# Attention and two MoE layers on one core: reciprocals a head later, transfers and opening in another order, the cosine's integer from ScalarE in the first block

## The chip, the cores and the metric

One core of a Trainium2 chip runs the whole program. The metric is the time of one execution in microseconds (us) on the device; lower is better. The kernel before takes 2205.02 us (median of three runs, 2204.62 to 2205.92).

## The reference

Three layers in a row, all in float32. Attention has 4 batches of 8 heads, 576 tokens of 64 numbers each, with a mask by blocks of 64. Its output, 2304 tokens of 512 numbers, goes through a layer with a cosine (512 to 2048 and back), and that through eight experts with a gate.

```python
scores = 0.125 * np.matmul(q, k.transpose(0, 1, 3, 2))
scores = np.where(mask, scores, -1e9)
attn = np.exp(scores - scores.max(-1, keepdims=True))
attn = attn / (attn.sum(-1, keepdims=True) + 1e-09)
x = np.matmul(attn, v)          # -> 2304 x 512
h = x @ w_in                    # first MoE
x = (h * np.cos(h)) @ w_out
...
for e in range(8):              # second MoE, P from a normalised gate
    out += P[:, e:e + 1] * (np.maximum(x @ w1[e], 0) @ w2[e])
```

## The kernel before

The whole program is written in a fixed order: each engine executes its instructions in the order in which the Python code records them, and waits on semaphores for the others. All transfers of the attention are issued by SyncE (SP in the profile), one after the other; an issue that has to wait holds up all behind it, and each waits until the eighth transfer ahead of it has landed.

**Attention** goes head by head (line 408, 32 heads). Precision is bought by splitting each float32 number into a high part and a low part. For head i the loop does, in this order: it evacuates the output of head i-1 from PSUM (`evac`, ScalarE) and sends its row of sums to DRAM (`sums`); it sends the high part of the next head's q to its place (`move_q_hi`, `qb<-qa`); TensorE makes the first half of the next head's peaks (`peak(i+1, 0)`, tile `px`) and VectorE finds their maxima (`find`, tile `nm`); TensorE makes the scores of head i (`weights`, tiles `sp`, `sq`, `sr`, `sc`), ScalarE their exponentials; then the second half of the peaks and its `find`. The two halves share one `px` in PSUM, so the second half waits for the first `find`. For head i+2, `high_parts` and `low_parts` split q and k, and `move_k_hi`, `move_k_lo` (`kb<-hi`, `kb<-qb`) send parts of k to other partitions. `move_q_hi` of a head overwrites what `move_k_lo` of it reads, so it waits for that transfer to land. Then come the products with v (`pv`, tile `o`), and between them the maxima of head i+1 are transposed (`turn`, tile `pt`) and written into `qa` (`maxima`, line 286); the scores of head i+1 wait for that.

Two heads make one pair, an even head and an odd one. The sums of a pair are fetched from DRAM in another layout (`fetch`, `sc<-sums`), inverted (`invert`, line 358, on VectorE), sent back (`give`), spread over the partitions (`spread`, `tt<-inv`), and the outputs are scaled by them (`scale`, one head each, line 375); `x_hi` on ScalarE and `x_lo` on GpSimd (POOL) split the result into `xh` and `xl`. `fetch`, `invert` stand in the even head, `give` and `spread` in the next odd one.

Beside this runs the conversion of the first MoE's weights from float64 to float32 (`Conv`, tiles `cw`, `tla`, `raw`): 32 halves, each in four steps, of which `some(n)` lets n run. Half of them run in the attention, one in each pair of heads, the rest in the first block of the first MoE.

**The first MoE** takes 3 blocks of 16 units. A unit makes two tiles of h (24 matmuls, `h<-xh,jh`), takes their cosine, and the unit after it multiplies the result by the second weights (`o_part`, `acc`). The cosine is ScalarE's Sin of h minus whole turns: `reduce_h` gets the integer `ki` and the rest `r` on VectorE, `sine` runs on ScalarE, `times` and `g_lo` on VectorE. Two tiles of h fit in PSUM, so a third waits for `times` of the first. The last pairs of the attention are finished in the first units (`leftover`). **The second MoE** follows from some 680 us to the end and is not touched.

## Time and profile before

| | |
|---|---|
| median of three runs | 2205.02 us |
| profiled execution, its own time | 2205.72 us |
| span of its trace, first to last instruction | 2203.9 us |
| TensorE, VectorE, ScalarE, GpSimd busy | 98%, 68%, 43%, 39% of the span |
| TensorE busy in the first two slices of 55 us | 7 and 8 tenths, then 8, 8, 8, 9 and 9 to the end |
| mean granted TensorE clock | 0.993 of full speed |

The profile's page has the busy shares of each engine, the span in 40 slices, the chain of work that ended last, and the costliest groups of instructions. Behind it stand views of the trace: windows of time with the busy time of each engine, the waits by engine and releaser, and the instructions in order of time.

### The profile page before, as it was taken

Reading aid. Unit: us, or ns where it says so; the run is one execution under the profiler, and the core shown is the slowest. Engines: PE = TensorE matmul, PEld = TensorE weight load, DVE = VectorE, ACT = ScalarE, POOL = GpSimd, SP = SyncE. Lnnn points to the kernel's source line nnn. Section 1 sums busy time; section 2 is a strip of 40 time slices with the busy share of each in tenths; the row PEclk is TensorE's granted clock in tenths of the full one; section 3 lists DMA queues with packets and bytes.
Section 4 is the critical chain, followed back from the end, with each engine's and each line's share of the span. In section 5 each row is a group of like instructions: output and inputs, shape, how many; then the busy total and the mean of one; then the engine's idle time right before and its main releaser. Section 6 shows DMA issues by size and latency. Waiting matters only on the chain.

```text
span 2203.9 us, 29623 instructions
## 1 busy us (share of the span) xinstructions
PE 2150.4 (98%) x10869; PEld 1889.4 (86%) x10869; DVE 1497.8 (68%) x2464; ACT 957.5 (43%) x1792; POOL 867.5 (39%) x766
## 2 busy tenths in 40 slices
PE   7888899999999999999999999999999999999999
PEld 5666689999898888888888888888888888888887
DVE  6777688666566876666767666666777666666665
ACT  5666555434444343433434434343434343433342
POOL 1222355333332343434563434343554343434341
PEclk9999999999999999999999999999999999999999
DMA  5676421000001121212122212121212221212120
GB/s 144 173 181 175 112 73 58 1 1 10 29 20 39 58 77 58 77 58 77 58 77 87 77 58 77 58 77 58 77 58 88 76 77 58 77 58 77 58 77 29
DMA packets 76641, 157.42 MB, mean 71 GB/s; under 512 B 33392, under 2 KB 33392, under 8 KB 76496
## 3 DMA queue, kind: packets, MB, share of 16 engines
q1 hardware_dynamic: 76496, 155.52, 23.1%
q8 instruction: 86, 1.41, 0.3%
q14 instruction: 59, 0.48, 0.1%
HBM read 136.91 MB, written 4.87 MB: 64 GB/s over the span
## 4 chain that ended last, share of the span: by engine, by line
PE 77%; DVE 7%; issue 7%; DMA 3%; ACT 3%; POOL 3%; SPq 1%; ACTq 0%; POOLq 0%; DVEq 0%
PE acc L470 12%; PE acc L472 12%; PE acc L471 12%; PE hx L472 6%; PE hx L470 6%; PE hx L471 6%; PE hy L472 3%; PE hy L470 3%; PE hy L471 3%; PE acc L701 3%; POOL jl L66 3%; DMA kb<-qb 1%; PE hz L470 1%; PE hz L472 1%; PE hz L471 1%
## 5 line engine op out<-in xcount | busy, mean ns | idle before, releaser
L580 POOL TENSOR_TENSOR wv<-stg,wv 128x512 fp32r<-128x512 f32 x190 | 333.7, 1778 | 858.5 <-ACT wv L579 858.5
L470 PE MATMUL acc<-wv,hh 128*128 128x512 f32 x1152 | 456.5, 396 | 0.0
L472 PE MATMUL acc<-wv,hl 128*128 128x512 f32 x1152 | 455.5, 395 | 0.0
L471 PE MATMUL acc<-wv,hh 128*128 128x512 f32 x1152 | 454.5, 395 | 0.0
L874 DVE SCALAR_TENSOR_TENSOR oa<-acc,P,oa 128x512 f32<-128x512 f32 x540 | 379.0, 740 | 4.9 <-PE acc L472 4.3
L845 ACT ACTIVATE hh<-c 128x384 fp32r<-128x384 f32 x288 | 151.4, 526 | 408.7 <-DVE c L930 167.8
L846 DVE SCALAR_TENSOR_TENSOR hl<-c,hh 128x384 fp32r<-128x384 f32 x288 | 164.0, 570 | 176.5 <-ACT hh L845 176.5
L472 PEld LDWEIGHTS acc<-wv,hl 128*128 128x128 f32 x1152 | 216.0, 187 | 53.7
L471 PEld LDWEIGHTS acc<-wv,hh 128*128 128x128 f32 x1152 | 215.9, 187 | 43.8
L470 PEld LDWEIGHTS acc<-wv,hh 128*128 128x128 f32 x1152 | 216.1, 188 | 43.0
L66 POOL TENSOR_TENSOR jl<-raw,jh 128x512 fp32r<-128x512 f32 x95 | 135.4, 1443 | 240.5 <-ACT jh L63 225.9
L923 DVE TENSOR_TENSOR c<-hz,c 128x384 f32<-128x384 f32 x96 | 53.5, 557 | 193.2 <-PE hz L472 193.2
L571 DVE TENSOR_TENSOR wal<-s,wah 128x1024 fp32r<-128x1024 f32 x96 | 171.4, 1785 | 0.0
L913 ACT ACTIVATE c<-hx 128x384 f32<-128x384 f32 x95 | 46.9, 493 | 275.5 <-PE hx L472 275.5
L470 PE MATMUL h<-xh,jh 128*128 128x384 f32 x384 | 130.5, 340 | 5.7 <-ACT jh L63 3.0
L472 PE MATMUL h<-xh,jl 128*128 128x384 f32 x384 | 129.9, 338 | 1.9 <-POOL jl L66 1.9
L673 ACT ACTIVATE r<-r,half_pi 128x384 f32<-128x384 f32 x96 | 59.2, 617 | 165.5 <-DVE r L668 164.7
L472 PE MATMUL hy<-xh,wal 128*128 128x384 f32 x384 | 128.8, 335 | 0.9 <-DVE wal L571 0.9
L471 PE MATMUL h<-xl,jh 128*128 128x384 f32 x384 | 129.2, 337 | 0.0
L470 PE MATMUL hx<-th,wah 128*128 128x384 f32 x384 | 128.6, 335 | 0.5 <-ACT c L913 0.5
L470 PE MATMUL hy<-xh,wah 128*128 128x384 f32 x384 | 128.7, 335 | 0.4 <-DVE c L930 0.2
L472 PE MATMUL hx<-th,wal 128*128 128x384 f32 x384 | 128.5, 335 | 0.0
(213 smaller groups left out, 4822.1 us busy)
## 6 DMA issues: line engine op xcount, KB each, us to landing
stg<-in_w_b_dram SPq DMA_DIRECT2D x192, 512.0 KB
cw<-in_w_a_dram SPq DMA_DIRECT2D x32, 512.0 KB
st<-in_qk_dram SPq DMA_DIRECT2D x64, 144.0 KB
v<-in_v_dram SPq DMA_DIRECT2D x31, 160.0 KB
tt<-inv SPq DMA_DIRECT2D x32, 144.0 KB
out_dram<-oa SPq DMA_DIRECT2D x18, 256.0 KB
kb<-hi SPq DMA_DIRECT2D x31, 144.0 KB
kb<-qb SPq DMA_DIRECT2D x31, 144.0 KB
```

The source lines that it names most:

```text
L66: eng_lo.tensor_tensor(out=lo, in0=src, in1=hi.bitcast(F32), op=ALU.subtract)
L470: nc.tensor.matmul(ps, lh, rh, start=first, stop=False, skip_group_check=go_on)
L471: nc.tensor.matmul(ps, lh, rl, start=False, stop=False, skip_group_check=go_on)
L472: nc.tensor.matmul(ps, ll, rh, start=False, stop=last, skip_group_check=go_on)
L571: eng.tensor_tensor(out=self.al, in0=self.s, in1=self.ah.bitcast(F32), op=ALU.subtract)
L580: eng.tensor_tensor(out=t[:, DM:2 * DM], in0=src, in1=t[:, 0:DM].bitcast(F32), op=ALU.subtract)
L673: nc.scalar.activation(r, r, AF.Sin, bias=half_pi)
L701: nc.tensor.matmul(acc[half, b][:, at:at + w_], w[:, s], h[:, t0:t0 + w_], start=f == 0 and i == 0 and at == 0, stop=f == F1 - 1 and i == ...
L845: nc.scalar.activation(hh, src, AF.Relu)
L846: nc.vector.scalar_tensor_tensor(out=hl, in0=src, scalar=0.0, in1=hh.bitcast(F32), op0=ALU.max, op1=ALU.subtract)
L874: nc.vector.scalar_tensor_tensor(out=o, in0=acc, scalar=p, in1=o, op0=ALU.mult, op1=ALU.add)
L923: nc.vector.tensor_tensor(out=c[0], in0=z, in1=c[0], op=ALU.add)
```

## The change

In the attention, `invert` and `give` move from the even head to the next odd head, behind the first `find`; `scale` of an even head moves to the end of the even head, `x_hi` and `x_lo` follow one head later, and a third buffer of outputs holds the pair that long. On SyncE's queue the loads of v, q and k come first in a head, then `sums` and `move_q_hi`; `fetch` and `spread` change places around `move_k_hi` and `move_k_lo`. The four steps of a conversion are cut differently. In the opening, GpSimd writes the constants of the second slot and the ones beside v, and VectorE makes `maxima(0)` ahead of `low_parts(1)`. The first weights of the first MoE are split during the last head, into a corner of `xh` and `xl` that is not yet written, and those of unit 1 ahead of unit 0. The left-over pairs are spread over units 1 to 9 instead of 0 to 5. In the 16 units of the first block, ScalarE makes the integer `ki`.

```diff
...
-            def constants(slots):
...
+            def constants(j, eng):
+                eng.tensor_copy(out=QA[j][:, 0:64], in_=diag[:, 0:64])
+                eng.tensor_copy(out=QA[j][64:96, 64:640], in_=diag[64:96, 64:640])
+                eng.tensor_scalar(out=KA[j][64:128, :], in0=diag[64:128, 0:S], scalar1=0.0, scalar2=None,
+                                  op0=ALU.mult)
...
+            def ones_of_v():
+                nc.gpsimd.memset(V[0][:, :, D:D + 1], 1.0)
+                nc.gpsimd.memset(V[1][:, :, 0:D], 0.0)
...
...
                 self.magnitude(k)
-                self.rounding(k)
                 if 0 < k < NHALF - 1:
                     self.load(k + 1)
                 yield
+                self.rounding(k)
                 self.clamp(k)
                 yield
                 self.shift(k)
+                self.bits(k)
                 yield
-                self.bits(k)
                 self.add(k)
                 yield
...
-            constants([0])
+            selectors()
+            constants(0, nc.vector)
+            constants(1, nc.gpsimd)
             first_head()
-            find(*peak(0, 0))
+            px = peak(0, 0)
+            tiles()
+            find(*px)
             find(*peak(0, 1))
-            constants([1])
             high_parts(1)
-            low_parts(1)
-            more_constants()
...
+            ones_of_v()
             turn(0)
             maxima(0)
+            low_parts(1)
...
                 if i:
                     evac(i - 1)
-                if odd and i >= 3:
-                    give(i - 3)
+                    if nxt:
+                        load_v(i + 1)
+                if i + 3 < NH:
+                    load(i + 3)
                 if i:
                     sums(i - 1)
+                if even and i:
+                    some(1)
                 if nxt:
                     move_q_hi(i + 1)
-                if i and nxt:
-                    load_v(i + 1)
-                if nxt:
                     find(*peak(i + 1, 0))
                 for part in range(4):
                     weights(i, part)
-                if i >= 4:
-                    scale(i - 4 - i % 2, i % 2)
+                if odd and i >= 3:
+                    invert(i - 3)
+                    give(i - 3)
+                if odd and i >= 5:
+                    scale(i - 5, 1)
                 if nxt:
                     find(*peak(i + 1, 1))
+                if nxt2:
+                    high_parts(i + 2)
+                    move_k_hi(i + 2)
+                if even and i >= 2:
+                    fetch(i - 2)
+                if nxt2:
+                    low_parts(i + 2)
+                    move_k_lo(i + 2)
                 if odd and i >= 3:
                     spread(i - 3)
-                if i + 3 < NH:
-                    load(i + 3)
-                if even and i >= 2:
-                    fetch(i - 2)
-                if i + 2 < NH:
-                    high_parts(i + 2)
-                    move_k_hi(i + 2)
-                    low_parts(i + 2)
-                    move_k_lo(i + 2)
-                if even:
-                    some(1)
-                elif i >= 5:
-                    x_hi(i - 5)
-                    x_lo(i - 5)
-                if even and i >= 2:
-                    invert(i - 2)
-                if odd:
-                    some(1)
+                if even and i >= 6:
+                    x_hi(i - 6)
+                    x_lo(i - 6)
+                if i == NH - 1:
+                    split(*spare, raw[0][:, 0:DM], nc.scalar, nc.gpsimd)
+                some(1)
                 pv(i, 0)
                 pv(i, 1)
...
                 for c in range(2, 5):
                     pv(i, c)
-                some(1)
+                if even and i >= 4:
+                    scale(i - 4, 0)
+                if odd:
+                    some(1)
...
-                    nc.vector.tensor_scalar(out=ki, in0=ps, scalar1=float(1 / TWO_PI), scalar2=0.25,
-                                            op0=ALU.mult, op1=ALU.add)
+                    if n < F1:
+                        nc.scalar.activation(ki, ps, AF.Identity, bias=quarter, scale=float(1 / TWO_PI))
+                    else:
+                        nc.vector.tensor_scalar(out=ki, in0=ps, scalar1=float(1 / TWO_PI), scalar2=0.25,
+                                                op0=ALU.mult, op1=ALU.add)
...
-                wsplit(0, 0, nc.vector)
+                wj[0, 0] = spare
...
+                        if n == 0:
+                            wsplit(1, 0)
```

What a pair of heads is on VectorE. First before: the end of an even head, from the step of the conversion that `bits` is, with the numbers of the tiles (`nm_106`, `qa_97` and so on are the two slots that even and odd heads use).

```order
L119 SCALAR_TENSOR_TENSOR raw<-cw,tla 128x512
L277 TENSOR_REDUCE nm_106<-px 128x1 x2
L375 TENSOR_TENSOR tt<-tla,tt 64x576
L277 TENSOR_REDUCE nm_106<-px 128x1 x3
L233 TENSOR_TENSOR qb_100<-st,hi 128x576
L358 RECIPROCAL sc_116<-sc_116 72x16
L286 TENSOR_TENSOR qa_97<-pt,diag 5x640
L108 TENSOR_SCALAR tla<-tla 128x512
```

Now VectorE with the change: from the maxima of an even head through the odd head after it.

```order
L296 TENSOR_TENSOR qa_101<-pt,diag 5x640
L385 TENSOR_TENSOR tt<-tla,tt 64x576
L287 TENSOR_REDUCE nm_109<-px 128x1 x2
L368 RECIPROCAL sc_121<-sc_121 72x16
L385 TENSOR_TENSOR tt<-tt 64x576
L287 TENSOR_REDUCE nm_109<-px 128x1 x3
L243 TENSOR_TENSOR qb_105<-st,hi 128x576
L113 TENSOR_SCALAR tla<-tla 128x512
L296 TENSOR_TENSOR qa_100<-pt,diag 5x640
L117 TENSOR_SCALAR tla<-tla 128x512
L124 SCALAR_TENSOR_TENSOR raw<-cw,tla 128x512
```

The reciprocal no longer stands ahead of the maxima of the same head; it stands one head later, behind the first `find`. Shift and bits of the conversion now follow the maxima of the odd head, and nothing of the conversion is left in the even head on VectorE.

What SyncE issues, before: an even head from its sums to the start of the next head.

```order
L352 DMA sums<-tt 1x576
L242 DMA qb_101<-qa_97 64x576
L194 DMA v_109<-in_v_dram 128x5x64
L185 DMA st<-in_qk_dram 64x576
L186 DMA st<-in_qk_dram 64x576
L355 DMA sc_116<-sums 72x2x8
L236 DMA kb_102<-hi 64x576
L239 DMA kb_102<-qb_100 64x576
L85 DMA cw<-in_w_a_dram 128x1024
L362 DMA inv<-sc_116 72x2x8
L352 DMA sums<-tla 1x576
L242 DMA qb_100<-qa_96 64x576
```

And SyncE with the change, an even head up to `fetch` and the conversion's load, and the start of the odd head.

```order
L200 DMA v_113<-in_v_dram 128x5x64
L191 DMA st<-in_qk_dram 64x576
L192 DMA st<-in_qk_dram 64x576
L362 DMA sums<-raw 1x576
L252 DMA qb_105<-qa_101 64x576
L246 DMA kb_106<-hi 64x576
L365 DMA sc_121<-sums 72x2x8
L249 DMA kb_106<-qb_104 64x576
L90 DMA cw<-in_w_a_dram 128x1024
...
L252 DMA qb_104<-qa_100 64x576
L372 DMA inv<-sc_121 72x2x8
```

The loads have moved ahead of `move_q_hi`, `fetch` has moved behind `move_k_hi`, and `give` (`inv<-sc`) has moved behind `move_q_hi` of the odd head.

## Rows read from the trace of the kernel before

**Rows 1.** Windows: us, busy PE, PEld, DVE, ACT, POOL, PEclk, DMA share, GB/s
```profile
36.88:250.22 213.34, 187.91 (x869) 133.21 (x869) 151.06 (x281) 132.53 (x235) 57.46 (x54) 0.94 0.67 173
121.70:127.70 6.00, 6.00 (x32) 4.16 (x32) 4.50 (x8) 5.16 (x9) 2.31 (x3) 1.00 0.55 136
127.70:138.33 10.63, 8.01 (x34) 6.03 (x32) 6.63 (x13) 4.58 (x8) 2.14 (x2) 0.84 0.80 218
```

**Rows 2.** Timeline, ScalarE: evacuations of heads 2 and 30 (start, us)
```profile
36.88 0.74 ACT L346 ACTIVATE tla<-o,eps 65x576 f32<-65x576 f32 x1 [0.30 <-PE o L340]
...
250.22 0.74 ACT L346 ACTIVATE tla<-o,eps 65x576 f32<-65x576 f32 x1 [1.73 <-PE o L340]
```

**Rows 3.** Waits of VectorE, 36.88 to 250.22 us: total us, times, longest
```profile
DVE sc L358 <- DMA sc<-sums: 42.8, 15, 4.9
```

**Rows 4.** Chain that ended last, 110 to 146 us: start, us
```profile
116.35 2.58 DMA qb<-qa
...
121.85 3.50 DMA kb<-qb
...
127.84 2.36 DMA sc<-sums
```

**Rows 5.** Timeline, TensorE, a head without a stall: its two peaks
```profile
121.70 0.82 PE L261 MATMUL px<-ka,qa 68*128 68x256 f32 x3
...
124.27 0.55 PE L261 MATMUL px<-ka,qa 68*128 68x256 f32 x3
```

**Rows 6.** Timeline, VectorE, the operations of a pair of heads
```profile
30.51 0.69 DVE L119 SCALAR_TENSOR_TENSOR raw<-cw,tla 128x512 int32<-128x512 int32 x1
...
120.24 0.42 DVE L112 TENSOR_SCALAR tla<-tla 128x512 int32<-128x512 int32 x1
...
121.56 1.04 DVE L119 SCALAR_TENSOR_TENSOR raw<-cw,tla 128x512 int32<-128x512 int32 x1
122.62 1.29 DVE L277 TENSOR_REDUCE nm<-px 128x1 f32<-128x448 f32 x2
...
124.85 0.89 DVE L277 TENSOR_REDUCE nm<-px 128x1 f32<-128x192 f32 x3 [0.26 <-PE px L261]
125.74 0.76 DVE L233 TENSOR_TENSOR qb<-st,hi 128x576 fp32r<-128x576 f32 x1
130.22 0.25 DVE L358 RECIPROCAL sc<-sc 72x16 f32<-72x16 f32 x1 [3.72 <-DMA sc<-sums]
130.50 0.83 DVE L286 TENSOR_TENSOR qa<-pt,diag 5x640 fp32r<-5x640 f32 x1
```

**Rows 7.** Timeline, GpSimd and ScalarE: low part of x, high part of q
```profile
120.64 1.40 POOL L382 TENSOR_TENSOR xl<-tt,xh 128x576 fp32r<-128x576 f32 x1 [1.50 <-ACT xh L378]
...
125.74 0.68 ACT L228 ACTIVATE qa<-st 64x576 fp32r<-64x576 f32 x1
```

**Rows 8.** Timeline of the opening: TensorE and GpSimd
```profile
8.12 0.66 POOL L229 CAST ka<-st 64x576 fp32r<-64x576 f32 x1
...
10.20 0.51 PE L282 MATMUL pt<-ident,nm 128*101 128x128 f32 x1 [1.07 <-DVE nm L277]
12.64 1.36 PE L261 MATMUL px<-ka,qa 68*128 68x256 f32 x3 [1.94 <-DVE ka L213]
...
16.58 0.79 PE L295 MATMUL sp<-qa,ka 101*128 101x512 f32 x1 [2.16 <-DVE qa L286]
```

**Rows 9.** Timeline, TensorE: the first matmul of the first MoE
```profile
258.36 0.69 PE L470 MATMUL h<-xh,jh 128*128 128x384 f32 x1 [3.01 <-ACT jh L63]
```

**Rows 10.** First block: starts of units on TensorE; one VectorE row
```profile
267.04 1.39 DVE L112 TENSOR_SCALAR tla<-tla 128x512 int32<-128x512 int32 x1
...
271.14 0.51 PE L701 MATMUL acc<-hh,jh 128*128 128x512 f32 x2
...
342.48 0.51 PE L701 MATMUL acc<-hh,jh 128*128 128x512 f32 x2
...
350.86 0.51 PE L701 MATMUL acc<-hh,jh 128*128 128x512 f32 x2
```

More of the change, by code (lines that the diff above doesn't have):

```diff
@@ L68, in attention_moe_kernel @@
     raw = [None] * F1
+    spare = [x[:, NC - 1, (B - 1) * S:(B - 1) * S + DM] for x in (xh, xl)]
     NHALF = 2 * F1
@@ L94, in magnitude @@
         def magnitude(self, k):
-            self.sc[k] = self.scratch(1, k, [128, DM])
+            self.sc[k] = self.own[1]
             nc.scalar.activation(self.sc[k].bitcast(F32), self.high(k).bitcast(F32), AF.Abs)
@@ L170, in attention @@
             tla = post.tile([128, 6 * TB], F32, tag="tl", name="tla", bufs=1)
-            RAW = [[tla[:, 2 * DM:2 * DM + S], p1.tile([128, S], F32, name="raw")],
-                   [tla[:, 2 * DM + S:2 * DM + 2 * S], tt[0][:, 0:S]]]
+            odd_raw = (post.tile([128, S], F32, tag="lt", name="rawl", bufs=1), p1.tile([128, S], F32, name="raw"),
+                       tt[0][:, 0:S])
+            RAW = [[tla[:, DM + j * S:DM + (j + 1) * S], odd_raw[j]] for j in range(3)]
             RB, XF = tt[1][:, 0:S], tt[2][:, 0:S]
-            conv = Conv(post.tile([128, 4 * DM], I32, tag="th", name="cw", bufs=1), tla[:, 0:2 * DM].bitcast(I32))
+            conv = Conv(post.tile([128, 4 * DM], I32, tag="th", name="cw", bufs=1), tla[:, 0:DM].bitcast(I32))
             conv_gen = conv.run()
@@ L198, in load_v, with selectors @@
                     nc.sync.dma_start(out=vt[0:64, 4, c], in_=v[b, h, 512:S, :])
[L200 removed]
+            def selectors():
                 nc.vector.memset(diag, 0.0)
[L202 to L203 removed]
                 shifted = diag[64:72, 64:576].rearrange("p (t h n) -> p t h n", h=2, n=64)
[L205 to L217 removed]
@@ L219, in more_constants, with step @@
-            def more_constants():
+                for h in range(2):
+                    nc.vector.tensor_copy(out=shifted[:, :, h, :], in_=step(1 - h))
+            def step(h):
+                return ident[64:72, 64 + 4 * h:68 + 4 * h].unsqueeze(2).to_broadcast([8, 4, 64])
+            def constants(j, eng):
[3 more added lines that the diff above has]
+                                  op0=ALU.mult)
+                for h in range(2):
+                    out = KA[j][64:72, 64:576].rearrange("p (t h n) -> p t h n", h=2, n=64)[:, :, h, :]
+                    eng.tensor_scalar(out=out, in0=step(1 - h), scalar1=MASK, scalar2=None, op0=ALU.mult)
+                eng.tensor_scalar(out=KA[j][96:101, :], in0=diag[96:101, 0:S], scalar1=-1.0, scalar2=None,
+                                  op0=ALU.add)
+                eng.memset(NM[j], 0.0)
@@ L374, in scale @@
                 r = slice(64 * h, 64 * h + 64)
-                nc.vector.tensor_tensor(out=XF[r, :], in0=RAW[e // 2 % 2][h][r, :], in1=RB[r, :], op=ALU.mult)
+                nc.vector.tensor_tensor(out=XF[r, :], in0=RAW[e // 2 % 3][h][r, :], in1=RB[r, :], op=ALU.mult)
             def x_hi(e):
@@ L408, in attention @@
             for i in range(NH):
[L409 removed]
+                nxt, nxt2, even, odd = i + 1 < NH, i + 2 < NH, i % 2 == 0, i % 2 == 1
                 if i:
                     evac(i - 1)
[L412 to L413 removed]
+                    if nxt:
+                        load_v(i + 1)
+                if i + 3 < NH:
+                    load(i + 3)
                 if i:
                     sums(i - 1)
+                if even and i:
+                    some(1)
                 if nxt:
                     move_q_hi(i + 1)
[L418 to L420 removed]
                     find(*peak(i + 1, 0))
@@ L454, in attention @@
                     pv(i, c)
-                some(1)
+                if even and i >= 4:
+                    scale(i - 4, 0)
+                if odd:
+                    some(1)
             evac(NH - 1)
+            sums(NH - 1)
             e = NH - 2
-            sums(NH - 1)
-            scale(e - 2, 0)
-            scale(e - 2, 1)
-            return conv_gen, {0: lambda: (x_hi(e - 2), fetch(e)), 1: lambda: (invert(e), give(e), x_lo(e - 2)),
-                              2: lambda: spread(e), 4: lambda: (scale(e, 0), scale(e, 1), x_hi(e)),
-                              5: lambda: x_lo(e)}
+            return conv_gen, {1: lambda: (x_hi(e - 4), x_lo(e - 4)), 2: lambda: scale(e - 2, 0),
+                              3: lambda: (scale(e - 2, 1), x_hi(e - 2), fetch(e)),
+                              4: lambda: (x_lo(e - 2), invert(e), give(e)), 5: lambda: spread(e),
+                              7: lambda: scale(e, 0), 8: lambda: (scale(e, 1), x_hi(e)), 9: lambda: x_lo(e)}
     with tc.manual_schedule():
```

43 lines of the change are left out of this document (14 added, 29 removed).

## The prediction

> **What bounds the kernel now.** I read the windows first, then the waits, then the instructions of single heads in order of time. From the first MoE on TensorE is hardly ever idle, so 0.2% of this kernel (4.4 us, about what a measurement can tell from no change) can only come from what lies before. The stretch between the evacuations of head 2 and head 30 [rows 2] is 14 pairs of heads in 213.34 us, 15.24 us a pair; TensorE is busy 187.91 of it, at a mean clock of 0.94 [rows 1]. A head without a stall takes 6.00 us with TensorE busy throughout at clock 1.00; the odd head behind it takes 10.63 us at 0.84 [rows 1]. So 12.00 us a pair is what TensorE needs, and 14 x 3.24 = 45.3 us are lost.
>
> The waits say to whom. VectorE stands 42.8 us in 15 waits for the fetched sums, all at the reciprocal [rows 3]. The next instruction on VectorE is the maxima (0.83 us), started 0.28 us after the reciprocal [rows 6], and TensorE's scores of the next head wait for them; TensorE idles 213.3 - 187.9 = 25.4 us in the stretch [rows 1]. The other 20 us of the 45.3 are slow matmuls: after such an idle the granted clock is lower, 0.84 in the stalled head and 1.00 in the one before [rows 1], that is, part of the time at 1.2 GHz and the rest at 2.4. A stall is paid nearly twice.
>
> **The change, part by part.**
>
> *The pairs of heads.* The reciprocal moves a head later. Its transfer is issued behind `move_k_hi`, which waits for the high part that ScalarE has done 4.0 us into a clean head, when that of q begins [rows 7]; with half a microsecond for that issue, an estimate, the fetch leaves at 4.6 and lands in 2.4 us in the row I have [rows 4]; its new turn is some 8.9 us after the even head's start (below), so it should find its data and cost its own 0.25 us [rows 6]. What is late next is VectorE itself, as it now has most of its work in the odd head. Take the even head's start (its first `px`) as 0. In a clean head the first `find` starts 0.92 us after it, and TensorE reaches the second `px` at 2.57 us [rows 5, 6]; that one needs the first `find` ended, and the v products stand behind it.
>
> Odd head, in its order: first `find` 1.29, reciprocal 0.25, scale 0.75 (as the low parts, of the same width), second `find` 0.9, low parts 0.75, clamp 0.42 (as the shift), maxima 0.83, shift 0.42, bits 0.69 to 1.04 [rows 6]: 6.3 to 6.7 us. Even head: 1.29 + 0.9 + 0.75 + 0.83 + 0.75 = 4.5 us. Together 10.8 to 11.2 us, under 12.0, but in the wrong places twice. The even head's scale must wait until GpSimd has read the same buffer: ScalarE's copy of x follows the high part of q, which ends 4.7 us into a clean head, and takes as long, 0.68 us [rows 7]: 5.4; GpSimd's 1.40 us [rows 7] end at 6.9, the scale at 7.6. The odd head has begun by then (6.0 to 6.35); its first `find` runs 7.6 to 8.9, and its second `px` is due at 6.35 + 2.57 = 8.9: just in time. The rest of the odd head runs back to back from 8.9: reciprocal 9.15, scale 9.9, `find` 10.8, low parts 11.55, clamp 12.0, maxima 12.8 (the next scores need them about a microsecond after the head's start, 13.3: in time), shift 13.3, bits 14.0. The next even head starts at 12.35; its first `find` ends at 15.3, 2.9 us into it instead of 2.2, and its second `px` comes 0.35 us late. That closes the cycle: **12.35 us a pair**, 12.7 with the bits at their slow 1.04 us [rows 6]. TensorE pauses for a third of a microsecond a pair, too little to bring the clock down as the 2 to 4 us stalls do.
>
> Then the transfers. SyncE moves the same bytes, 173 GB/s x 15.24 us = 2.64 MB a pair, in less time: 208 GB/s at 12.7 us. One stretch shows 218 GB/s with a share of 0.80 [rows 1], so they fit, but with less room. The chain that matters is `kb<-qb`, then `qb<-qa`, which may only be issued when the first has landed: 2.58 us for one transfer in the quick row and 3.50 in the slow one [rows 4]. With the change `qb<-qa` stands behind three loads and is issued about 2.5 us into a head; with the slow 3.50 us it lands at 6.0, and the scores that need it start about 0.7 us into the next head, when the first `px` are through [rows 5]. Nothing is lost, with 0.7 us to spare. I take the upper of my two values, 12.7 us, since both slow rows are likelier in a denser stretch: 14 x (15.24 - 12.7) = **-35.6 us**. Bounds: 12.0 (TensorE alone), -45.4, and 13.7 (a full microsecond a pair lost to transfers), -21.6.
>
> *The opening.* VectorE ends the second `find` of head 0 about 10.1 us in, but makes the constants of slot 1, low parts and more before `maxima(0)`, so the transposed maxima of 10.20 wait and the scores start at 16.58 [rows 8]. Now those constants are GpSimd's. What stays ahead of these scores on TensorE are the peaks of head 1, 12.64 us now, and one more matmul, which come straight after the transpose (ends 10.71) if slot 1 is ready: 10.7 + 1.8 = 12.5, a gain of 4.1 at best. GpSimd took the copy of 64x576 in 0.66 us [rows 8] and has seven such or smaller pieces ahead of its part in head 0, 3 to 4.6 us, with room until about 5.2. What can spoil it is that VectorE writes its own constants in the same microseconds. Where the two overlap, the shift that takes 0.42 us took 1.39 [rows 6, 10]. If half of GpSimd's 3.3 us fell on VectorE, it would lose 1.6; I take a third, 1.1: **-3.0 us**, bounds -4.1 and -0.8 (all of the 3.3).
>
> The Trainium skill, "SBUF — State Buffer", section "SBUF: two separate sides", speaks against this part: VectorE and GpSimd share one pair of ports, held by whichever starts first for a whole instruction, and "the other fully blocks". The 1.39 us row agrees with it. By that rule alone VectorE would lose the 3.3 us wholly, the opening would give 0.8 instead of 3.0, and the time would be 2.2 us higher.
>
> *The seam to the first MoE.* Its first matmul waits 3.01 us, for a split that was queued behind the last scale [rows 9]; the split now runs in the last head. After the idle the first nine matmuls come 0.32 us apart instead of 0.17, so 1.5 us more go to the clock. **-4.5 us**, bounds -3.0 and -4.5. Units 0 and 1 keep their own wait for `times`, as no `acc` lies between them; the gate's load and ScalarE's table load now stand in that chain, and I cost this at nothing.
>
> *The first block.* From 271.14 to 342.48 us eight units take 71.34, where a clean unit takes 8.38 [rows 10]: 4.3 us lost, where the left-over pairs meet the conversion on VectorE. Now each left-over step has a unit of its own, and two operations a unit of about 0.55 us leave VectorE for ScalarE, which is half idle there. In clean units that is worth nothing, as TensorE is the bound and the o_part matmuls hide the longer chain over two engines; if that cover went, the price would be some 0.2 us a unit for the hops. I take **-2.5 us**, bounds 0 and -4.3. Four scales instead of two now fall into this block, each beside spare time of VectorE.
>
> Sum: -35.6 - 3.0 - 4.5 - 2.5 = -45.6 us against the span of 2203.9, 2158.3; the execution lies 1.8 us above its span and the median 0.7 below that execution, so the median comes to **2159 us**. All bounds at their best give -58.3 (2147), all at their worst -25.4 (2180).
>
> **The rivals.**
>
> *TensorE is the only bound.* If GpSimd and bits come quicker than above, pairs take 12.0 us: -45.4 - 10.0 = -55.4, 2150 us. For it: VectorE needs only 10.8 of 12.0 us. Against it: the odd head alone needs more than its 6.0.
>
> *The transfers bind.* Ahead of `qb<-qa` in the odd head now stand the conversion's 512 KB, v and two loads, 960 KB in all, 4.5 us at 218 GB/s [rows 1]. If that makes it land some 0.7 us past its slack, a pair takes 13.4 us: -25.8 - 10.0 = -35.8, 2169 us. For it: the 3.50 us row at a high share; against it: pairs that took 12.8 us before kept up.
>
> *Half of it.* The reciprocal finds its data late in some pairs and the clock falls again there; 14.3 us a pair, -13.2 - 10.0 = -23.2, 2182 us.
>
> *Slower.* The reciprocal now stands ahead of the second `find`, the low parts and the maxima of the odd head; if its data came late, it would hold up not only the next scores but also `kb<-qb` and with it `qb<-qa`. The point from which the kernel loses: a pair must exceed 15.24 + 10.0 / 14 = 15.95 us, 3.6 above 12.35. The fetch has 4.3 us until its turn, so it would have to land 7.9 us after its issue, against 2.36 [rows 4] and a longest wait of 4.9 at a much earlier turn [rows 3]. At 16.5 us a pair it would be +17.6 - 10.0 = +7.6, 2213 us.
>
> **How the numbers follow.** My forecast 0.50 (its own range 2152 to 2165), TensorE alone 0.15, transfers 0.25, half 0.05, slower 0.03; 0.02 that stalls in other places leave it within 4.4 us of now. Range 2147 to 2178: it takes in the first three cases with their bounds, and leaves out some 1 in 10. Faster by over 0.2%: 0.50 + 0.15 + 0.25 + 0.05 = 0.95; same 0.02; slower 0.03.
>
> **What would show it.** In the profile after: no long wait of VectorE at the reciprocal; evacuations 6.0 and 6.4 to 6.7 us apart by turns; the granted clock of the attention at 0.98 or more, against 0.94; the first `h` matmul within 0.5 us of the last `o`, and at full clock; attention's end near 217 us instead of 255. TensorE's idle should be short and in front of the second `px`; if it lies in front of `sp` and ends with `qb<-qa`, the transfers bind. Waits of VectorE at the reciprocal that last longer than 1 us would make the prediction wrong, as would a low clock without such waits.

## The result and the profile after

The changed kernel takes 2183.73 us (median of four runs, 2182.47 to 2187.2); the kernel before took 2205.18 beside it, a ratio of 0.9905 (95% interval 0.9888 to 0.9922). The gain is 21 us where 46 were forecast, and the time lies above the range. The span is 2181.7 us instead of 2203.9.

The stretch of the 14 pairs in the changed kernel (windows; columns as in [rows 1]) and the evacuations of heads 2, 30 and 31 (timeline, ScalarE):

```profile
33.84:226.26 192.42, 180.81 (x869) 124.64 (x870) 148.39 (x278) 132.60 (x236) 55.77 (x54) 0.98 0.77 190
```

```profile
33.84 0.74 ACT L356 ACTIVATE tla<-o,eps 65x576 f32<-65x576 f32 x1 [0.85 <-PE o L350]
...
226.26 0.74 ACT L356 ACTIVATE tla<-o,eps 65x576 f32<-65x576 f32 x1 [2.21 <-PE o L350]
...
231.43 0.74 ACT L356 ACTIVATE rawl<-o,eps 128x576 f32<-128x576 f32 x1 [1.46 <-PE o L350]
```

A pair takes 13.74 us, against 15.24 before and 12.7 in the forecast. The idle time of TensorE in the stretch fell from 25.4 to 11.6 us and the clock rose from 0.94 to 0.98. The waits of the stretch, VectorE and TensorE (total us, times, longest), say what went and what came:

```profile
DVE tt L385 <- POOL xl L392: 8.8, 10, 1.1
...
DVE sc L368 <- DMA sc<-sums: 0.3, 1, 0.3
```

```profile
PE sp L304 <- DMA qb<-qa: 9.1, 11, 1.5
```

VectorE's 42.8 us at the reciprocal [rows 3] are 0.3 now: that part went as forecast. Of TensorE's 11.1 us of waits 9.1 end with the high part of q, as one rival said they would. The chain that ended last has that transfer at two lengths (start, us):

```profile
92.83 4.78 DMA qb<-qa
...
101.64 2.65 DMA qb<-qa
...
107.19 4.78 DMA qb<-qa
```

Behind an even head's own loads (448 KB) it takes 2.65 us here, near the 2.58 of [rows 4]. In the odd heads shown it takes 4.78. Eight of the 11 waits (6.9 us) lie in odd heads, with transfers of 4.06 to 4.78 us; three (2.2 us) lie in even heads, with 2.43, 2.65 and 3.79 us. SyncE's timeline shows what stands ahead of it in an odd head, and TensorE's the start of that head (its first `px`) and what the transfer costs:

```profile
104.34 0.54 SPq L90 DMA_DIRECT2D cw<-in_w_a_dram  x1
104.98 0.40 SPq L200 DMA_DIRECT2D v<-in_v_dram  x1
105.48 0.49 SPq L191 DMA_DIRECT2D st<-in_qk_dram  x1
106.03 0.59 SPq L192 DMA_DIRECT2D st<-in_qk_dram  x1
106.71 0.39 SPq L362 DMA_DIRECT2D sums<-tla  x1
107.19 0.48 SPq L252 DMA_DIRECT2D qb<-qa  x1
```

```profile
103.11 0.82 PE L271 MATMUL px<-ka,qa 68*128 68x256 f32 x3
...
112.02 0.50 PE L304 MATMUL sp<-qb,kb 128*128 128x512 f32 x1 [1.24 <-DMA qb<-qa]
```

The conversion's load of 512 KB, v and two loads, 960 KB in all, were issued within the 2.9 us before it. `qb<-qa` itself was issued 4.08 us into the head, where the forecast had 2.5, and landed 8.9 us into it. Over the stretch the issue comes 3.5 us into the odd heads and 4.7 us into the even ones (medians). While it is under way the transfer engines also move the two transfers of k, issued at 108.37 and 109.22 us (windows):

```profile
105.00:112.00 7.00, 5.78 (x30) 4.01 (x28) 6.80 (x14) 4.51 (x8) 1.71 (x2) 1.00 0.94 222
```

The seam (TensorE's two waits, VectorE and ScalarE in the same microseconds):

```profile
237.84 0.41 PE L482 MATMUL h<-xh,jh 128*128 128x384 f32 x1 [2.09 <-DVE g L692]
...
241.73 0.44 PE L482 MATMUL h<-xh,jh 128*128 128x384 f32 x1 [1.54 <-DVE g L692]
```

```profile
234.31 1.03 DVE L69 CAST ghl<-g 128x32 fp32r<-128x32 f32 x1 [4.97 <-DMA g<-in_gate_dram]
```

```profile
234.31 1.28 ACT L688 ACT_TABLE_LOAD   x1
```

The wait of 3.01 us [rows 9] and the slow matmuls behind it are gone. In their place unit 0's cosine waits for the gate's load on VectorE and the table on ScalarE; TensorE's same two waits for `g` were 0.49 and 0.90 us before. From the evacuation of head 31 to the first `acc` it is 243.91 - 231.43 = 12.48 us (before 271.14 - 255.39 = 15.75).

The first block, by its first and twelfth `acc` on TensorE, and by one wait in it:

```profile
243.91 0.39 PE L716 MATMUL acc<-hh,jh 128*128 128x512 f32 x1
...
279.15 0.45 PE L482 MATMUL h<-xh,jh 128*128 128x384 f32 x1 [1.55 <-DVE g L692]
...
345.15 0.51 PE L716 MATMUL acc<-hh,jh 128*128 128x512 f32 x2
```

That is 101.24 us for eleven units, 9.1 over 11 x 8.38; before it was 4.3 over [rows 10]. Between 225 and 400 us VectorE's longest total of waits is for the integer that ScalarE now makes, and what it does ahead of the late `g` of that row is this (timeline, VectorE):

```profile
DVE r L683 <- ACT ki L679: 27.5, 23, 2.6
```

```profile
275.25 0.55 DVE L683 SCALAR_TENSOR_TENSOR r<-ki,h 128x384 f32<-128x384 int32 x1 [1.06 <-ACT ki L679]
275.72 1.49 DVE L700 TENSOR_TENSOR hl<-g,hh 128x384 fp32r<-128x384 f32 x1
277.13 1.50 DVE L113 TENSOR_SCALAR tla<-tla 128x512 f32<-128x512 f32 x1
278.55 0.55 DVE L692 TENSOR_TENSOR g<-h,r 128x384 f32<-128x384 f32 x1
```

The integer came 1.06 us after VectorE was free for it, so `hl` and the conversion's clamp fell together with two long operations of GpSimd (timeline, POOL):

```profile
275.49 1.30 POOL L130 TENSOR_TENSOR raw<-raw,cw 128x512 int32<-128x512 int32 x1
276.75 1.59 POOL L70 TENSOR_TENSOR jl<-raw,jh 128x512 fp32r<-128x512 f32 x1
```

The opening (TensorE's first transpose, the scores that need the maxima and the first products with v; two constants on GpSimd; one constant and one wait on VectorE):

```profile
13.27 0.51 PE L292 MATMUL pt<-ident,nm 128*101 128x128 f32 x1 [1.07 <-POOL v L234]
...
15.14 0.63 PE L305 MATMUL sp<-qa,ka 101*128 101x512 f32 x1
...
18.47 1.02 PE L338 MATMUL o<-ep,v 128*65 128x512 f32 x2
```

```profile
2.94 1.76 POOL L218 TENSOR_SCALAR ka<-diag 64x576 fp32r<-64x576 bf16 x1
4.78 2.36 POOL L222 TENSOR_SCALAR ka<-ident 8x256 fp32r<-8x256 f32 x2
```

```profile
3.10 0.91 DVE L218 TENSOR_SCALAR ka<-diag 64x576 fp32r<-64x576 bf16 x1
...
8.89 0.81 DVE L228 CAST diag<-ident 5x640 bf16<-5x640 f32 x1 [2.00 <-POOL ka L223]
```

In the kernel before, the same constant on VectorE and the same products on TensorE:

```profile
2.57 0.44 DVE L210 TENSOR_SCALAR ka<-diag 64x576 fp32r<-64x576 bf16 x1
```

```profile
20.43 1.91 PE L328 MATMUL o<-ep,v 128*65 128x512 f32 x2
```

The transpose comes 3.07 us later than in [rows 8], but the scores that need the maxima follow it after 1.87 us instead of 6.38. They start 1.44 us earlier than before (15.14, and 16.58 in [rows 8], which is the same product). From there to its evacuation head 0 takes 6.49 us instead of 8.07, with TensorE busy throughout in both: above all the first products with v take 1.02 us instead of 1.91. The trace's first record of the granted clock, at full speed, begins at 17.98 us, and at 22.58 in the kernel before. A lower clock ahead of it would fit, but isn't shown.

### The profile page after: what moved, and what is told of

Read it like the earlier page. It is cut to its first block, busy times and chain, and to the rows that moved or that the text cites. A ratio compares the mean times of both kernels' runs of the same rounds, so it can differ in the third digit from the quotient of the medians.

```text
span 2181.7 us, 29633 instructions
## 1 busy us (share of the span) xinstructions
PE 2140.5 (98%) x10869; PEld 1878.7 (86%) x10869; DVE 1475.5 (68%) x2418; ACT 973.0 (45%) x1824; POOL 873.1 (40%) x777
## 4 chain that ended last, share of the span: by engine, by line
PE 77%; issue 7%; DVE 6%; ACT 3%; POOL 3%; DMA 3%; SPq 0%; ACTq 0%; POOLq 0%; DVEq 0%
PE acc L482 12%; PE acc L484 12%; PE acc L483 12%; PE hx L484 6%; PE hx L482 6%; PE hx L483 6%; PE hy L484 3%; PE hy L482 3%; PE hy L483 3%; PE acc L716 3%; POOL jl L70 3%; DMA qb<-qa 2%; PE hz L482 2%; PE hz L483 1%; PE hz L484 1%
## 5 line engine op out<-in xcount | busy, mean ns | idle before, releaser
L483 PE MATMUL hy<-xl,wah 128*128 128x384 f32 x384 | 128.3, 334 | 0.0
L483 PE MATMUL hx<-tl,wah 128*128 128x384 f32 x384 | 128.3, 334 | 0.0
```

The costliest lines, as they stand in the source:

```text
L483: nc.tensor.matmul(ps, lh, rl, start=False, stop=False, skip_group_check=go_on)
```

## The experiments

The theory: the pairs lack a microsecond because `qb<-qa` of the odd head stands behind the conversion's load; the block lost time by the integer on ScalarE. The rivals: SyncE's queue itself, VectorE's odd head with its wait for GpSimd's low part, and for the block the new spread of the left-over pairs. The kernel before took medians from 2200.3 to 2206.3 us beside the different groups of runs, so runs of different groups are compared by their ratios to it, or by the pair in the trace (evacuations of heads 2 and 30). e3 and e4 leave the attention as it is in the changed kernel and show 13.58 and 13.66 us a pair, so 0.15 us between two traces says nothing. The intervals of e1, e2, e3, e4, e6, e10 and e17 overlap the changed kernel's: what these runs show rests on their traces.

| run | median us | ratio to before (95%) | us a pair |
|---|---|---|---|
| changed kernel | 2183.73 | 0.9905 (0.9888 to 0.9922) | 13.74 |
| e13 no load of the conversion | 2170.01 | 0.9853 (0.9838 to 0.9867) | 12.67 |
| e14 the same, VectorE's work divided otherwise | 2169.58 | 0.9852 (0.9837 to 0.9866) | 12.77 |
| e10 VectorE's work divided otherwise | 2184.27 | 0.9918 (0.9903 to 0.9933) | 13.84 |
| e1 `move_q_hi` first | 2179.89 | 0.9881 (0.9866 to 0.9895) | 13.59 |
| e2 load behind `move_q_hi`, even head | 2187.62 | 0.9913 (0.9898 to 0.9928) | 13.91 |
| e15 load behind `move_q_hi`, odd head | 2191.28 | 0.9950 (0.9933 to 0.9967) | 14.25 |
| e17 load in two pieces | 2179.85 | 0.9904 (0.9889 to 0.9919) | 13.39 |
| e6 give and spread issued by GpSimd | 2177.70 | 0.9884 (0.9868 to 0.9901) | 13.22 |
| e3 integer on VectorE | 2179.78 | 0.9882 (0.9866 to 0.9899) | 13.58 |
| e4 gate after unit 2 | 2183.66 | 0.9897 (0.9883 to 0.9912) | 13.66 |
| e5 before, only the reciprocal moved | 2221.24 | 1.0084 (1.0069 to 1.0099) | 16.29 |
| e11 e6 + e3 + e4 | 2171.05 | 0.9856 (0.9841 to 0.9870) | 13.24 |

**The load left out (e13), and with VectorE relieved as well (e14).**

```diff
-                if 0 < k < NHALF - 1:
+                if 0 < k < F1:
+                    self.w64[k + 1] = self.scratch(0, k + 1, [128, DM, 2])
+                elif 0 < k < NHALF - 1:
                     self.load(k + 1)
```

> The changed kernel without the conversion's 512 KB load in the attention (15 loads left out; the conversion runs on the two halves loaded at the start, so the first MoE's weights are not the reference's). Theory (the bytes and the place of this load in front of qb<-qa make the missing microsecond of a pair): pairs of 12.7 to 12.9 us, qb<-qa under 3.5 us in the chain, 2183.7 - 14 x 0.9 = about 2171 us. Rival (SyncE's in-order queue and the issue of 19 transfers a pair make it, not the bytes): pairs of 13.4 us or more, 2179 us or more.

> The same without the load, with VectorE's work of a pair divided otherwise as in the run of that alone. Theory (two limits behind one another, transfers first, then VectorE's wait for the low part): with the transfers out of the way the division now pays, pairs of 12.2 to 12.5 us (TensorE alone needs 6.00 + 6.21), 5 to 8 us under the run without the load. Rival (TensorE's order of matmuls keeps the odd head at 6.7 us whatever VectorE does): within 2 us of that run.

The stretch without the load (windows), and an odd head, an even one and the next odd one in it:

```profile
34.06:211.48 177.42, 175.02 (x869) 123.58 (x870) 148.07 (x278) 132.46 (x236) 56.47 (x54) 1.00 0.69 164
```

```profile
122.73:128.94 6.21, 6.21 (x32) 4.69 (x32) 5.92 (x12) 4.52 (x8) 1.00 (x2) 1.00 0.69 159
128.94:135.03 6.09, 6.09 (x32) 4.18 (x33) 4.63 (x9) 5.08 (x10) 2.81 (x3) 1.00 0.72 187
135.03:141.69 6.66, 6.49 (x32) 4.62 (x33) 5.95 (x11) 4.49 (x9) 1.22 (x2) 1.00 0.59 137
```

12.67 us a pair, the forecast's 12.7, at full clock, and no wait for `qb<-qa` is left. Of the 15.0 us that the stretch lost to the load, 9.2 were idle (11.6 against 2.4) and 5.8 slower matmuls (180.81 against 175.02 busy). The rival of the queue alone falls: SyncE issued 18 of its 19 transfers a pair, in the same order. With the load gone `qb<-qa` is also issued earlier, 2.7 us into the odd heads and 3.4 us into the even ones (medians), so this run doesn't part the load's bytes from what the load holds up in the queue. The rows also correct a number: an odd head takes TensorE 6.21 us at full clock, not 6.00. Dividing VectorE's work otherwise (below) adds nothing even here, as the rival of e14 had it: in e14 even heads take 6.0 us and most odd ones 6.7, and the wait has moved from `px` to `pt`.

**VectorE's work divided otherwise (e10).**

```diff
-                if even and i:
-                    some(1)
...
                     find(*peak(i + 1, 0))
+                if even and i:
+                    some(2)
...
                 if odd and i >= 5:
+                    scale(i - 5, 0)
                     scale(i - 5, 1)
...
-                if even and i >= 4:
-                    scale(i - 4, 0)
-                if odd:
-                    some(1)
+            some(1)
```

> The changed kernel with only VectorE's work of a pair divided otherwise (shift, bits and add behind the first find of the even head, both scales in the odd head). Theory (VectorE's wait for GpSimd's low part and its full odd head cost 0.4 to 0.7 us a pair): 2174 to 2178 us, pairs 13.0 to 13.3 us, the waits of VectorE's scale for the low part gone. Rival (transfers alone bind): 2181 to 2185 us, pairs 13.6 to 13.8 us, TensorE's waits for qb<-qa as long as before (9 us).

The waits for the low part are gone, the pair is no shorter and TensorE's waits for `qb<-qa` are 10.7 us. My theory of this run fell, its rival held: GpSimd's low part cost nothing while the transfers bound.

**Moving the transfers (e1, e2, e15, e17).**

First e1, then e15 (e2 has `if even and i:` there), then e17, whose `load` takes the half as a second argument.

```diff
                 if i:
                     evac(i - 1)
-                    if nxt:
-                        load_v(i + 1)
-                if i + 3 < NH:
-                    load(i + 3)
...
                     move_q_hi(i + 1)
+                if i and nxt:
+                    load_v(i + 1)
+                if i + 3 < NH:
+                    load(i + 3)
...
```

```diff
-                if 0 < k < NHALF - 1:
+                if F1 <= k < NHALF - 1:
                     self.load(k + 1)
...
                     move_q_hi(i + 1)
+                if odd and i >= 3:
+                    conv.load(i // 2 + 1)
...
```

```diff
-                    self.load(k + 1)
+                    self.load(k + 1, 0 if k < F1 else None)
...
                     move_k_lo(i + 2)
                 if odd and i >= 3:
+                    conv.load(i // 2 + 1, 1)
```

> The changed kernel with the high part of q sent ahead of the loads of v, q and k in each head, as in the kernel before; nothing else undone. Theory A (the transfer that feeds the scores is late because it queues behind the loads, 960 KB in an odd head): the qb<-qa transfer takes 2.5 to 3.5 us instead of up to 4.8, TensorE's 9 to 11 us of waits for it go, a pair of heads takes 12.7 to 13.0 us instead of 13.74, and the time falls by 10 to 14 us to about 2171. Rival B (the transfer engines are full, whatever the order): another transfer becomes the late one, pairs stay at 13.5 to 13.9 us, time within 3 us of 2183. Rival C (SyncE now stands still waiting for kb<-qb before it may issue qb<-qa, and the loads get late): pairs of 14 us or more, 2187 or more.

> The changed kernel with the 512 KB load of the conversion issued in the even head behind the high part of q instead of at the head's end, so that it is no longer ahead of the odd head's qb<-qa; the loads of v, q and k stay ahead of it. Theory A: the long qb<-qa transfers of the odd heads fall from 4.1 to 4.8 us to about 3.5, pairs take 13.0 to 13.3 us, the time falls by 6 to 10 us to about 2175. Rival B (full engines): kb<-hi and kb<-qb of the even head get late instead, time within 3 us of 2183.

> The changed kernel with the conversion's load issued in the odd head, straight behind move_q_hi, where SyncE then waits some 2 us for the high part of k; the same bytes. Theory (the place of the load matters, not its bytes): qb<-qa of the odd head under 3.5 us, no wait for it over 0.5 us, the fetch in the even head untouched, pairs of 12.8 to 13.1 us, about 2173 us. Rival (the bytes matter, and the load makes the next transfers late, as it did in the even head): kb or the spread come late instead, pairs of 13.5 us or more, 2181 us or more.

> The changed kernel with the conversion's load in two pieces of 256 KB: one where it stood at the end of the even head, one in the odd head behind move_k_lo; the same bytes, one issue more. Theory (the bytes that stand ahead of qb<-qa in one head make it late, and they queue): the piece in front of each qb<-qa is half as large, so it takes about 4.7 - 256 KB / 200 GB/s = 3.4 us; pairs of 12.8 to 13.2 us, 2171 to 2176 us. Rival (the pair's transfers as a whole are what binds): some qb<-qa are late in both heads, pairs of 13.6 us or more, 2181 us or more.

Each order made something else late. In e1 TensorE's waits for `qb<-qa` fell to 2.2 us, but the fetch came late for the reciprocal (13.5 us of VectorE's waits, up to 2.4 each), and TensorE waited in other places. In e2 they fell to 0.5, and the fetch took 3.7 to 4.7 us: TensorE waited 10.6 us to transpose the maxima that VectorE finds behind the reciprocal. In e15 the chain and SyncE's waits (34 to 226 us) show a third way:

```profile
180.06 3.95 DMA inv<-sc
184.02 2.41 DMA tt<-inv
187.55 3.29 DMA qb<-qa
```

```profile
SPq L377 <- DMA inv<-sc: 25.1, 12, 2.7
```

`inv<-sc`, 4.5 KB, takes 3.95 us behind the load (1.91 in e13); the issue of `spread` waits for it, and the loads and `move_q_hi` of the next head stand behind that issue. So the theory of e15 fell and its rival held. With two pieces (e17) the pair is 0.35 us shorter than in the changed kernel, 0.2 shorter than in e3. Where TensorE waits for it `qb<-qa` takes 2.6 to 4.5 us, and 16 waits (9.9 us) stand where there were 11 (9.1 us), as it is still issued 4.2 us into the odd heads and 4.5 us into the even ones (medians). By the ratio the run is level with the changed kernel. So both theories of e17 hold in part: the bytes in front of one `qb<-qa` matter, and so does the pair's traffic as a whole.

**SyncE's queue (e6).** `give` and `spread` of the head loop are issued by GpSimd.

```diff
...
-                    give(i - 3)
+                    give(i - 3, nc.gpsimd)
...
-                    spread(i - 3)
+                    spread(i - 3, nc.gpsimd)
```

> The changed kernel with the reciprocals' way back and their spreading (3 of the 19 transfers of a pair, and the one wait for a transfer of about 1.2 us) issued by GpSimd instead of SyncE in the attention. Theory J (SyncE's queue binds: 9.4 us of issues a pair plus its waits in order): the others are issued earlier, qb<-qa starts up to 2 us earlier in the even head, pairs fall to 12.9 to 13.2 us, time falls by 7 to 11 us to about 2174. Rival B (the transfer engines' load binds): transfers issued earlier only queue longer, pairs stay within 0.2 us of 13.74, time within 3 us of 2183. Rival K (the issues on GpSimd hold up its casts and hold the ports against VectorE): 2186 or more.

The pair falls to 13.22 us and SyncE's 16.8 us of waits for `inv<-sc` are gone; TensorE's waits for `qb<-qa` fall from 9.1 to 5.1. The queue carried about half of the missing microsecond, with the load in place. `qb<-qa` is issued 2.9 us into the odd heads and 2.5 us into the even ones (medians). But where TensorE waits for it, it takes 4.4 to 5.8 us, also in four even heads, where the conversion's load isn't ahead of it: part of what the queue gives back goes into longer transfers, as Rival B said.

**The first block (e3) and the seam (e4).**

```diff
-                    if n < F1:
+                    if n < 0:
                         nc.scalar.activation(ki, ps, AF.Identity, bias=quarter, scale=float(1 / TWO_PI))
```

```diff
-                gate_prep()
                 last = NU - F1
...
+                    if n == 2:
+                        gate_prep()
                     if n in leftover:
```

> The changed kernel with the cosine's integer on VectorE in the first block too, as before. Theory D (the integer on ScalarE queues behind the high part of the result before it and so makes the chain from h to the product longer): the excess of units 0 to 12 in the first block, 9.1 us over 8.38 us a unit now, falls to 3 to 5 us, and the time falls by 4 to 6 us to about 2178. Rival E (the left-over scales in units 2, 3, 7 and 8 make the excess): it stays at 8 us or grows, as VectorE has more to do, time within 2 us of 2183 or above.

> The changed kernel with the gate's weights prepared on VectorE at the end of unit 2 instead of ahead of unit 0. Theory F (VectorE waits 5.0 us for the gate's load with the first rest r behind it, and units 0 and 1 stall for that): the waits of 2.09 and 1.54 us in unit 1 fall to 0.5 to 1.3 in all, the time falls by 2 to 3 us to about 2181. Rival G (ScalarE's table load and its order make the same wait): they fall by less than 1 us, time the same.

With the integer on VectorE the first and the twelfth `acc` start here:

```profile
242.93 0.51 PE L716 MATMUL acc<-hh,jh 128*128 128x512 f32 x2
...
339.87 0.51 PE L716 MATMUL acc<-hh,jh 128*128 128x512 f32 x2
```

96.94 us, 4.8 over clean pace: ScalarE's integer cost 4.3 us, and the new spread of the left-over pairs gained nothing (4.3 before). The ten traces with the integer on ScalarE take 101.2 to 103.3 us for these eleven units, the eight with it on VectorE 96.9 to 98.1. In e3 the seam is 0.6 us longer instead (13.12 us). The edit of e4 moves the four instructions of `gate_prep` on VectorE; the gate's load and ScalarE's table load stay where they stand in the program. In e4 head 31 to the first `acc` takes 11.62 us instead of 12.48, and waits of 1.20 and 1.57 us stay, with the table load still in unit 0's chain. The gate was worth 0.9 us there; the block behind it takes 103.30 us, 2.1 more, so the total does not show it.

**The reciprocal alone (e5).** The kernel before, with only `invert` and `give` moved.

```diff
-                if odd and i >= 3:
-                    give(i - 3)
...
                     weights(i, part)
+                if odd and i >= 3:
+                    invert(i - 3)
+                    give(i - 3)
...
-                if even and i >= 2:
-                    invert(i - 2)
```

> The kernel before with one thing of the change: the reciprocal and its transfer back stand in the odd head behind the first find, as in the changed kernel; the order of transfers, the opening and the first MoE are those of before. Theory H (the reciprocal's stall was worth most of the 45 us, and what keeps the changed kernel at 13.74 us a pair is the order of transfers that came with it): pairs take 12.7 to 13.2 us, time 2165 to 2173. Rival I (with the stall gone, any order meets the next bound, SyncE's queue and the transfers, at 13.5 us or more a pair): pairs take 13.5 to 14.2 us, time 2180 to 2192.

Slower by 18 us, and 16.29 us a pair, which neither theory foresaw. VectorE's waits, 36.68 to 264.70 us:

```profile
DVE qb L233 <- ACT hi L227: 24.8, 14, 2.3
DVE tt L375 <- DMA tt<-inv: 20.0, 12, 3.4
DVE sc L358 <- DMA sc<-sums: 15.6, 13, 1.7
```

The old scale, ahead of the second `find`, now has its inverse late. In the changed kernel the move of the reciprocal comes with a new place of the scale, a third buffer and a new order of transfers; which of these makes it pay no run shows.

**Joined.** e11 takes e6, e3 and e4 together.

> The changed kernel with give and spread issued by GpSimd, ki on VectorE in the first block, and the gate's load and table after unit 2; VectorE's work of a pair as in the changed kernel. Theory (three separate losses, each in its own stretch, that add): 2177.7 - 4.0 - 0.5 = about 2173 us; pairs 13.2 us, the first block 97 us from its first to its twelfth acc. Rival (the conversion and the left-over work shift the loss from one to the other): 2177 us or more.

It is the quickest that leaves nothing out: 0.9856 (0.9841 to 0.9870), clear of the changed kernel's interval, as its theory said. (Here too the edit leaves the gate's load and the table load where they stand in the program.) It also shows what the rest of the seam was. With the integer no longer ahead of it on ScalarE, the table load starts 1.28 us after the evacuation of head 31 (2.88 in the changed kernel), and the seam takes 235.43 - 224.55 = 10.88 us (timeline, ScalarE and TensorE):

```profile
224.55 0.74 ACT L356 ACTIVATE rawl<-o,eps 128x576 f32<-128x576 f32 x1 [1.46 <-PE o L350]
...
225.83 1.28 ACT L688 ACT_TABLE_LOAD   x1
```

```profile
235.43 0.51 PE L716 MATMUL acc<-hh,jh 128*128 128x512 f32 x2
```

The other joins came out no better. e1 + e3 + e4: 0.9865 (0.9851 to 0.9880), within the interval of e11; the same with e6: 0.9876.

> The changed kernel with three of the tried parts together: the high part of q first, the integer on VectorE in the first block, the gate's weights after unit 2. If the parts add: -2 to -3 us from the attention, -4 from the block, -1 to -2 from the seam: 2174 to 2177. If the first block's two parts hide each other: 2178 to 2180.

> The same three parts, and the reciprocals' way back and spreading issued by GpSimd. Theory J: another 7 to 11 us below the version without that, about 2166. Rival B: the same as that version. Rival K: above it.

e11 with e10's division: 0.9871; that with `move_q_hi` first: 0.9872.

> The changed kernel with give and spread issued by GpSimd, ki on VectorE in the first block, the gate's load and table after unit 2, and VectorE's work of a pair divided otherwise: shift, bits and add of the conversion right behind the first find of the even head, both scales of a pair in the odd head (the even head's scale then no longer waits for GpSimd's low part). Theory (transfers and VectorE's odd head both cost, and their gains add): 2176.4 span of the queue alone, less 4 (ki), less 1 (gate), less 14 x 0.5 (balance): about 2165 us; pairs about 12.7 us, odd heads 6.2 us. Rival (transfers alone bind, VectorE has room): no less than 2171 us, pairs 13.2 us.

> As the run with all four parts, and in addition move_q_hi ahead of the loads on SyncE's queue, as in the kernel before. Theory (with give and spread off that queue, the loads ahead of move_q_hi are the last thing that makes it late): 3 to 5 us less than the run with all four, waits of TensorE for qb<-qa under 1 us in all. Rival (what q gains the fetch and k lose): within 2 us of it, with waits for pt or px in place of qb<-qa.

e11 with the load in the odd head: 0.9871; with the load in two pieces: 0.9884.

> The conversion's load in the odd head, with give and spread issued by GpSimd, ki on VectorE in the first block, and the gate's load and table after unit 2. Theory (these add): 2171.0 of the three without the load moved, less 14 x 0.4: about 2166 us. Rival (the load in its new place collides): 2171 us or more.

> The load in two pieces, with give and spread issued by GpSimd, ki on VectorE in the first block, and the gate's load and table after unit 2. Theory (the gains add): 2171.0 of the three without the pieces, less 14 x 0.4: 2164 to 2167 us, pairs of 12.8 us. Rival (with the queue relieved the pieces move nothing): 2170 us or more.

With the load's bytes in place the gains of orders don't add: pairs stay between 13.1 and 13.8 us in these six joins, and apart from the first of them the time came out as the rivals had it. The last two have the shortest pairs (13.10 and 13.12 us) and lose it at the seam (13.90 and 12.31 us), where TensorE waits 2.13 and 1.62 us for GpSimd's part of the first split (0.17 in e11).

## Why the prediction was wrong, point by point

The forecast's span was 2158.3 us, the measured one 2181.7: 23.4 more. By the traces 14.7 of it lie in the pairs, 7.3 in the block, 1.2 in the seam, and none in the opening.

- **What bounds it.** Right: VectorE's wait for the sums went, and with it part of the slow clock (0.94 to 0.98; TensorE's busy time fell by 7.1 us in the stretch, and by another 5.8 in e13).
- **VectorE's and TensorE's cycle, 12.35 to 12.7 us a pair.** Right as a sum (12.67 in e13), but partly by luck. TensorE alone needs 12.21, not 12.00, so the rival of 12.00 could not happen; it idles 0.17 us a pair in e13, not a third of a microsecond; and without the wait for GpSimd's low part (e14) the pair is no shorter.
- **The transfers.** This is the step that failed: "with the slow 3.50 us it lands at 6.0 ... Nothing is lost, with 0.7 us to spare". Both of its terms were short. The slow row was that of another transfer, `kb<-qb`, at another place of the queue; behind 960 KB `qb<-qa` took 4.1 to 4.8 us where TensorE waited for it. And "issued about 2.5 us into a head" became 3.5 us in odd heads and 4.7 in even ones, as issues and waits stand ahead of it on SyncE. So -35.6 became -20.9. The rival "the transfers bind" had the place and the bytes right, and 13.4 us where 13.74 came; the bound of 13.7 was nearly the result. The trace of before held a reason to distrust 3.5: 960 KB at its 218 GB/s take 4.5 us. That this comes near 4.78 is partly luck, as the first of these bytes were issued 2.9 us earlier and the transfers of k shared the engines.
- **The block.** "-2.5 us" was +4.8. The step that failed is "In clean units that is worth nothing, as TensorE is the bound and the o_part matmuls hide the longer chain over two engines": each integer became a handover, VectorE waited 27.5 us in 23 of them, and its work came late beside GpSimd's. e3 gives 4.3 us of it to the integer, 0.4 a unit where I had priced the hops at 0.2 "if that cover went"; the left-over pairs' new places changed nothing.
- **The seam.** -4.5 was -3.3. "I cost this at nothing" failed: units 0 and 1 waited 2.09 and 1.54 us, before 0.49 and 0.90. e4 takes back 0.9, and with the integer off ScalarE as well (e11) the seam is 4.9 us shorter than before: the gate's work and, behind unit 0's integer, the table load made the difference.
- **The opening.** -3.0 came as -3.04 (evacuation of head 2 at 33.84, before 36.88), and that is luck. The order gave 1.44: GpSimd's constants took 0.66 + 1.76 + 2.36 + 1.65 us, twice my 3.3. Beside them VectorE's own four took 3.33 us instead of 1.84, so it lost 1.5 where I had taken 1.1, and it waited another 2.00 us until GpSimd had read `diag`, a wait for a buffer that the forecast did not have. The other 1.6 came from quicker matmuls in head 0, which it did not have either. The rule of the Trainium skill, "SBUF — State Buffer", section "SBUF: two separate sides", is borne out in part. VectorE is slower beside GpSimd, here and in the block (1.49 and 1.50 us), but in the opening it was not blocked for GpSimd's whole instruction: its constant begun at 3.10 us ended at 4.01, while GpSimd's, begun at 2.94, ran to 4.70.
- **Slower.** The rival's mechanism is what e5 shows, at the scale (20.0 us) as well as at the reciprocal (15.6 us); in the changed kernel the data were there (0.3 us).

What stays open is how the rest of the microsecond in e6 and e17 divides between late issues and engines shared with other transfers.

## What to carry to other kernels

A transfer's time in a quiet stretch is no price for it behind other transfers: look at the bytes issued around it and at when the queue gets to issue it, and do both for the head in which the largest load falls. When a wait on the critical engine goes, an in-order queue of transfers can be the next limit, and moving one transfer in it moves the wait; leaving a load out shows in one run what it costs. Splitting a short chain over two engines to relieve one that wasn't the bound bought handovers here.

## What the runs showed of the hardware

The same transfer of 144 KB, `qb<-qa`, took 2.65 us behind 448 KB of loads (3.79 in another head) and 4.78 us behind 960 KB, and a 4.5 KB one 1.91 us without the conversion's load and 3.95 us behind it. GpSimd took 1.76 us for a constant of 64x576 while VectorE took 0.91 for its own; in the kernel before, with GpSimd idle, VectorE had made it in 0.44. A constant of 5x576 took GpSimd 1.65 us with VectorE idle, and VectorE 0.46 in the kernel before.
